# K and V transfers that read HBM in pieces of 48 KB and write rows of 24 KB

## The chip, the cores and the metric

The kernel runs on one core of a Trainium2 chip. The metric is the time of one execution on the device, in microseconds. Runs of one kernel agree within about 0.1%.

## The reference

Four attention blocks run one after the other (A, B, A, B), each for a single new token against a cache of 8192 keys. There are 32 heads of 192 elements, the model width is 640, and everything is bf16.

```python
def block(x, k_cache, v_cache, wq, wo):            # x: 1 x 1 x 640
    q = layernorm(x) @ wq                          # 32 heads of 192
    scores = einsum("bhqd,bhkd->bhqk", q, k_cache) * 192 ** -0.5   # 8192 keys a head
    o = einsum("bhqk,bhkd->bhqd", softmax(scores), v_cache)
    return x + o @ wo                              # wo: 6144 x 640
# x = A(x); x = B(x); x = A(x); x = B(x)
```

Each head of each block needs 3 MB of K and 3 MB of V once. That is 805 MB in 256 transfers, and the weights wq and wo add 63 MB.

## The kernel before

Every engine has a list of instructions with explicit semaphores. For each head, the SyncE queue loads K into one of three buffers and V into one of three others. A buffer is 128 partitions x 24 KB, so each partition holds 64 keys. VectorE multiplies K by the head's query and sums it (ScalarE sums 8 of the 64 rows). After the softmax, TensorE multiplies with V and then with wo.

```python
def sp_k(h, Kt=Kt):
    i = counters["k"] % NKSLOT                 # three buffers
    counters["k"] += 1
    SP.wait(T["kslot"][i])                     # until the buffer's last reader is done
    def f(s, i=i, h=h):
        return s.dma_start(kslot[i][:, :], Kt[0, h].rearrange("(p j) d -> p (j d)", p=128))
    return i, SP.op(f, sem=semK[i], inc=16)
# sp_v is the same for V
...
def sp_wo(g, WO=WO):                           # 768 rows of wo, for four heads
    ...
        return s.dma_start(wo_buf[s_][:, 0:NT, :], WO[r0:r0 + NT * 128, :].rearrange("(t p) n -> p t n", p=128))
...
JA = min(JJ, cfg.get("act_rows", 8))           # rows of the 64 that ScalarE sums
```

## Time and profile before

| | before |
|---|---|
| time, median | 2074.88 us |
| DMA queue of the loads, share of 16 engines | 99.3% |
| VectorE busy | 1764.8 us (85%) |
| HBM read over the span | 868 MB at 419 GB/s |

These lines are from the page of the kernel before. The first rows are the span and each engine's busy time. The DMA row gives the busy share of the DMA engines in tenths, in forty equal slices, and the GB/s row gives what they moved. The packet line, the queue of the loads, and one group of VectorE follow. The last two lines are issues of K and V, with their median time from issue to landing in us.

```profile
span 2073.2 us, 24389 instructions
...
PE 1158.3 (56%) x9625; PEld 915.1 (44%) x9668; DVE 1764.8 (85%) x1190; ACT 596.1 (29%) x3254; POOL 3.1 (0%) x13
...
DMA  9999999999999999999999999999999999999995
GB/s 395 430 425 428 422 422 427 426 430 419 423 426 425 427 422 424 426 426 428 418 423 426 423 429 424 422 427 426 426 410 425 425 423 424 423 423 425 426 427 254
DMA packets 77813, 869.79 MB, mean 420 GB/s; under 512 B 4994, under 2 KB 29572, under 8 KB 44932
...
q1 hardware_dynamic: 77700, 868.24, 99.3%
...
L463 DVE TENSOR_TENSOR kslot<-kslot,q_sb 128x12288 bf16<-128x12288 bf16 x128 | 839.3, 6557 | 226.2 <-DMA kslot<-in_A_k_cache_dram 116.6
...
kslot<-in_A_k_cache_dram SPq DMA_DIRECT2D x64, 3072.0 KB, 32.6
vslot<-in_A_v_cache_dram SPq DMA_DIRECT2D x64, 3072.0 KB, 36.1
...
```

The DMA engines are busy in every slice but the last. A transfer lands 33 to 36 us after it was issued, while moving 3 MB takes about 7.3 us (an estimate: 3.15 MB at the 431 GB/s that stretches with K and V packets alone show). So four or five transfers are always queued, and the engines hardly ever lack work.

The view of the waits of the same kernel (who waited for whom: us in total, times, longest) shows that VectorE waits for K:

```profile
...
DVE kslot L463 <- DMA kslot<-in_A_k_cache_dram: 116.6, 56, 8.2
DVE kslot L463 <- DMA kslot<-in_B_k_cache_dram: 96.6, 49, 6.8
...
```

The trace also records every DMA packet. Over all records of the queue of the loads, sorted by size:

```
kernel  bytes   packets   median ns   sum / 16 engines, us
before  24576     32768         915                 1881.2   K and V
before   2048     15360          87                   85.2   wq
before   1280     24578          58                   90.5   wo
```

One packet of K or V is 24 KB, a whole row of a partition. There are 128 per transfer, so eight for each of 16 engines if they are dealt evenly (the records name no engine).

### The profile page before, as it was taken

The numbers are of one execution on the slowest core, as the hardware profiler recorded it, in microseconds if no ns is written. First come the engines' busy times: TensorE is split into PE (matmuls) and PEld (weight loads), VectorE is DVE, ScalarE is ACT, GpSimd is POOL, SyncE is SP. The second block draws the span as 40 slices with busy tenths as digits, with TensorE's granted clock in tenths as the row PEclk, the third lists the DMA queues.
The fourth block names the chain that finished last, engine by engine and source line by source line (L and its number), as shares of the span: only waits on it lengthen the run. The fifth ranks groups of instructions, "written<-read, shape, count | busy, mean of one in ns | idle before, by whom it ended". The sixth has DMA issues, their size and how long they took to land.

```text
span 2073.2 us, 24389 instructions
## 1 busy us (share of the span) xinstructions
PE 1158.3 (56%) x9625; PEld 915.1 (44%) x9668; DVE 1764.8 (85%) x1190; ACT 596.1 (29%) x3254; POOL 3.1 (0%) x13
## 2 busy tenths in 40 slices
PE   2565556555465555566536565556563665556656
PEld 1444444444354444444425454445452454444444
DVE  7888888988698888898779888889878988888896
ACT  2222232232232322232223332223222332223232
POOL 0000000000000000000000000000000000000000
PEclk7777777877678777777767777777776777777877
DMA  9999999999999999999999999999999999999995
GB/s 395 430 425 428 422 422 427 426 430 419 423 426 425 427 422 424 426 426 428 418 423 426 423 429 424 422 427 426 426 410 425 425 423 424 423 423 425 426 427 254
DMA packets 77813, 869.79 MB, mean 420 GB/s; under 512 B 4994, under 2 KB 29572, under 8 KB 44932
## 3 DMA queue, kind: packets, MB, share of 16 engines
q1 hardware_dynamic: 77700, 868.24, 99.3%
q8 instruction: 76, 1.25, 0.2%
q14 instruction: 37, 0.30, 0.0%
HBM read 868.22 MB, written 0.00 MB: 419 GB/s over the span
## 4 chain that ended last, share of the span: by engine, by line
DMA 45%; issue 25%; DVE 24%; PE 4%; ACT 1%; SPq 1%; POOL 0%; POOLq 0%; DVEq 0%; ACTq 0%
DMA kslot<-in_B_k_cache_dram 28%; DMA kslot<-in_A_k_cache_dram 17%; DVE kslot L463 12%; DVE kslot L504 5%; DVE kslot L492 4%; PE OB L557 3%; DVE s_sb L508 1%; SPq L312 0%; DVE M_sb L530 0%; DVE m_sb L515 0%; PE QB L412 0%; PE YL L632 0%; ACT p_sb L547 0%; DVE rl_sb L572 0%; SPq L295 0%
## 5 line engine op out<-in xcount | busy, mean ns | idle before, releaser
L463 DVE TENSOR_TENSOR kslot<-kslot,q_sb 128x12288 bf16<-128x12288 bf16 x128 | 839.3, 6557 | 226.2 <-DMA kslot<-in_A_k_cache_dram 116.6
L557 PE MATMUL OB<-vslot,p_sb 128*1 128x192 bf16 x8192 | 951.1, 294 | 84.3 <-ACT p_sb L547 78.6
L557 PEld LDWEIGHTS OB<-vslot,p_sb 128*1 128x1 bf16 x8192 | 809.6, 101 | 205.7 <-ACT p_sb L547 93.5
L539 PE MATMUL SA<-M_bf,ones_bf 1*128 1x1 bf16 x128 | 22.9, 179 | 689.2 <-ACT M_bf L537 689.2
L504 DVE TENSOR_TENSOR kslot<-kslot 128x2688 bf16<-128x2688 bf16 (+2 forms) x384 | 374.4, 975 | 13.3
L492 DVE TENSOR_TENSOR kslot<-kslot 128x5376 bf16<-128x5376 bf16 x128 | 374.7, 2927 | 0.1
L481 ACT ACTIVATE kslot<-kslot 128x192 bf16<-128x192 bf16 x1024 | 355.3, 348 | 22.2 <-DVE kslot L463 22.2
L539 PEld LDWEIGHTS SA<-M_bf,ones_bf 1*128 1x128 bf16 x128 | 12.4, 97 | 725.0 <-ACT M_bf L537 725.0
L537 ACT ACTIVATE M_bf<-M_sb 1x1 bf16<-1x1 f32 x128 | 26.5, 207 | 666.3 <-DVE M_sb L530 666.3
L481 ACT ACTIVATION_READ_ACCUMULATOR kslot<-kslot 128x1 f32 x1024 | 192.1, 188 | 0.0
L508 DVE TENSOR_REDUCE s_sb<-kslot 128x56 f32<-128x672 bf16 x128 | 109.1, 852 | 4.4
L632 PE MATMUL YL<-wo,oT_sb 128*1 128x512 bf16 x256 | 83.0, 378 | 51.8 <-ACT oT_sb L609 31.7
L605 ACT ACTIVATE oT_sb<-OB 128x1 bf16<-128x1 f32 x64 | 11.2, 175 | 310.9 <-PE OB L593 310.9
L608 ACT ACTIVATE oT_sb<-OB 64x1 bf16<-64x1 f32 x64 | 10.9, 170 | 281.0 <-PE OB L597 281.0
L412 PE MATMUL QB<-wq,xT_b 128*128 128x512 bf16 x197 | 57.5, 426 | 11.2 <-issue 6.4
L523 PE MATMUL SA<-ident,m_bf 128*1 128x128 bf16 x128 | 28.2, 221 | 54.5 <-ACT m_bf L520 54.5
L632 PEld LDWEIGHTS YL<-wo,oT_sb 128*1 128x1 bf16 x256 | 20.7, 81 | 79.7 <-ACT oT_sb L609 37.2
L634 PE MATMUL YH<-wo,oT_sb 128*1 128x128 bf16 x256 | 55.9, 218 | 0.0
L425 ACT ACTIVATE q_sb<-QB 128x512 bf16<-128x512 f32 x48 | 28.7, 598 | 93.6 <-PE QB L412 93.6
L578 ACT ACTIVATE orow_bf<-OB,rl_sb 1x192 bf16<-1x192 f32 x128 | 51.0, 399 | 1.7 <-DVE rl_sb L572 1.7
L547 ACT ACTIVATE p_sb<-s_sb,negm_sb 128x64 bf16<-128x64 f32 x128 | 44.8, 350 | 4.1
L530 DVE TENSOR_REDUCE M_sb<-SA 1x1 f32<-1x128 f32 x128 | 34.7, 271 | 12.6 <-PE SA L523 12.6
(50 smaller groups left out, 368.9 us busy)
## 6 DMA issues: line engine op xcount, KB each, us to landing
kslot<-in_A_k_cache_dram SPq DMA_DIRECT2D x64, 3072.0 KB, 32.6
vslot<-in_A_v_cache_dram SPq DMA_DIRECT2D x64, 3072.0 KB, 36.1
kslot<-in_B_k_cache_dram SPq DMA_DIRECT2D x64, 3072.0 KB, 32.6
vslot<-in_B_v_cache_dram SPq DMA_DIRECT2D x64, 3072.0 KB, 36.3
wq<-in_A_wq_dram SPq DMA_DIRECT2D x12, 1280.0 KB, 24.9
wo<-in_A_wo_dram SPq DMA_DIRECT2D x16, 960.0 KB, 38.2
wq<-in_B_wq_dram SPq DMA_DIRECT2D x12, 1280.0 KB, 25.7
wo<-in_B_wo_dram SPq DMA_DIRECT2D x16, 960.0 KB, 38.6
```

What stands on the lines that cost most here:

```text
L412: return t.matmul(QB[nb % 2][:, 0:ncols], lhsT=xT_b[:, c, :], rhs=wq_buf[s_][:, c, (nb % 2) * 512:(nb % 2) * 512 + ncols], start=(c == 0), ...
L463: e = DV.op(lambda v, k3=k3, qb_ap=qb_ap: v.tensor_tensor(k3, k3, qb_ap, ALU.mult))
L481: ea = AC.op(lambda a, k3=k3, par=par, j=j: a.activation(k3[:, j, :], k3[:, j, :], ACT.Copy, accum_out=s_sb[par][:, j:j + 1]))
L492: e = DV.op(lambda v, kt=kt, hw_=hw_: v.tensor_tensor(kt[:, :, 0:hw_], kt[:, :, 0:hw_], kt[:, :, hw_:DH], ALU.add))
L504: e = DV.op(lambda v, kt=kt, hw_=hw_, w=w: v.tensor_tensor(kt[:, :, 0:hw_], kt[:, :, 0:hw_], kt[:, :, hw_:w], ALU.add))
L508: cur["s"] = DV.op(lambda v, kt=kt, par=par, w=w, JA=JA: v.tensor_reduce(s_sb[par][:, JA:JJ], kt[:, :, 0:w], AX.X, ALU.add))
L539: cur["negM"] = PE.op(lambda t, par=par: t.matmul(SA[par][:, SA_NEGM:SA_NEGM + 1], lhsT=ones_bf[0:1, 0:128], rhs=M_bf[par][0:1, 0:1], star ...
L547: cur["p"] = AC.op(lambda a, par=par: a.activation(p_sb[par][:], s_sb[par][:], ACT.Exp, bias=negm_sb[par][:], scale=C))
L557: return t.matmul(OB[par][0:1, 0:DH], lhsT=p_sb[par][:, j:j + 1], rhs=vs3[:, j, :], start=(j == 0), stop=(j == JJ - 1))
L578: cur["orow"] = AC.op(lambda a, par=par: a.activation(orow_bf[par][:], OB[par][0:1, 0:DH], ACT.Copy, scale=rl_sb[par][0:1, 0:1]), tag=(f"O ...
L632: return t.matmul(YL[0:1, 0:512], lhsT=lhsT, rhs=rhs[:, 0:512], start=st, stop=sp_)
L634: return t.matmul(YH[0:1, 0:D - 512], lhsT=lhsT, rhs=rhs[:, 512:D], start=st, stop=sp_)
```

## The change

The source of a K or V transfer is described as 64 rows of 48 KB, while the destination keeps 128 rows of 24 KB. Row r of the source is what goes to partitions 2r and 2r + 1, so every byte lands where it did. The author built the instruction by hand. The intent is half as many pieces to read, and with them less fixed cost.

```diff
--- before.py
+++ after.py
@@ -113,6 +113,13 @@
         return bad
 
 
+def wide(nc, e, out, in_):
+    inst = mybir.InstDMACopy(mode="Copy", name=nc.get_next_instruction_name(), engine=e.engine,
+                             ins=list(e.lower_ap_dma(in_)), outs=list(e.lower_ap_dma(out)),
+                             queue="qSPDynamicHW", ant_dge_precooked=False)
+    return e.add_instruction(inst)
+
+
 def build(nc, A_x, A_k, A_v, A_wq, A_wo, B_x, B_k, B_v, B_wq, B_wo, out, dbg=None, cfg=None):
     cfg = dict(cfg or {})
     dbg = dict(dbg or {})
@@ -309,7 +316,7 @@
                 counters["k"] += 1
                 SP.wait(T["kslot"][i])
                 def f(s, i=i, h=h):
-                    return s.dma_start(kslot[i][:, :], Kt[0, h].rearrange("(p j) d -> p (j d)", p=128))
+                    return wide(nc, s, kslot[i][:, :], Kt[0, h].rearrange("(p j) d -> p (j d)", p=64))
                 return i, SP.op(f, sem=semK[i], inc=16)
 
             def sp_v(h, Vt=Vt):
@@ -317,7 +324,7 @@
                 counters["v"] += 1
                 SP.wait(T["vslot"][i])
                 def f(s, i=i, h=h):
-                    return s.dma_start(vslot[i][:, :], Vt[0, h].rearrange("(p j) d -> p (j d)", p=128))
+                    return wide(nc, s, vslot[i][:, :], Vt[0, h].rearrange("(p j) d -> p (j d)", p=64))
                 return i, SP.op(f, sem=semV[i], inc=16)
 
             ev_wq = [None] * NPAIR
```

## The prediction

> **What bounds the kernel.** The DMA engines do. On the profile's page the DMA row of the forty slices reads 9 throughout until the last slice, the DMA queue of the K/V/weight loads is busy for 99.3% of 16 engines' span, and 868 MB at 419 GB/s is the whole span of 2073 us. VectorE, the next busiest, is at 1765 us (85%). The longest real wait of VectorE is for K transfers (116.6 + 96.6 us in the waits view). K and V are 256 transfers of 3 MB, 805 MB, 93% of the bytes. They land 32.6 to 36.3 us after issue, 4 to 5 times what one takes to move, so the queue is always several transfers deep.
>
> The trace's packet records show how little is left: 32768 packets of 24576 B (8 per engine per transfer), median 915 ns, summing to 1881 us per engine. Stretches in which only such packets run move 430.6 GB/s (median), 428.5 (mean). [...] Packets of 2048 B take 87 ns and those of 1280 B 58 ns. A line through the three sizes gives about 0.0368 ns per byte plus about 11 ns a packet (estimate).
>
> **What the change does.** The bytes, their order and their places are the same: rows of 48 KB in HBM are two neighbouring partitions of 24 KB. Each engine reads 4 pieces instead of 8 and still writes 8. If a packet goes with a read piece, 256 x 4 = 1024 packets fewer per engine at about 10 to 11 ns each: some 10 us off the DMA time. If the fixed part goes with the write side, nothing. Nothing is added on VectorE, TensorE or ScalarE. The hand-built instruction may take the SyncE queue a little longer to issue (0.33 us shortest now), but that queue waits over 1 ms for free buffers, so this is hidden.
>
> **Critical path.** The DMA stream runs without gaps from about 2 to 2058 us, so nearly all of what it saves shows in the span; the last 15 us (last head's compute, output) stay. VectorE at 13.8 us a head keeps up with 16.0. I expect 9 us less: 2066 us, range 2056 to 2086. Over 2% faster is nearly excluded[...]: chance 0.02. Within 2%: 0.80. Slower by over 2%: 0.18.
>
> **What would make it wrong.** [...] Fewer than 16 engines [...] I don't expect. [...]
>
> **What the profile would show.** Right: DMA packets drop from 77813 to about 61400, K/V packets are 48 KB and take about 1820 ns; pure K/V stretches run at about 433 GB/s; the DMA row stays 9; VectorE busy stays 1765 us and its waits for K fall by some 10 us; K landing falls slightly. Wrong by no effect: packets fewer, but each over 1830 ns, GB/s unchanged at 424. [...]

On the sum: 1024 packets fewer for each engine at about 10 to 11 ns (estimate from the packet times 915, 87 and 58 ns) came to some 10 us, and the forecast was 9 us less, 2066 us.

## The result

The time is 2074.98 us (median of 4 runs, 2074.16 to 2075.83), against 2074.78 us for the kernel before in the same rounds. The ratio is 0.9999, with a 95% interval of 0.9985 to 1.0013. Ratios here are the mean time of one kernel's fast runs over that of the other's of the same rounds, so they are not quite the ratio of the quoted medians. The interval leaves room for a gain of 3 us, not for 9.

The same lines of the page of the changed kernel (its line numbers are 7 higher):

```profile
span 2072.3 us, 24432 instructions
...
PE 1157.5 (56%) x9668; PEld 912.9 (44%) x9668; DVE 1765.3 (85%) x1190; ACT 593.2 (29%) x3254; POOL 3.1 (0%) x13
...
DMA  9999999999999999999999999999999999999995
GB/s 395 431 430 427 423 424 426 424 429 415 425 427 428 429 421 422 428 428 423 419 427 425 422 425 422 422 428 425 423 421 423 428 422 421 426 422 428 426 425 255
DMA packets 61429, 869.79 MB, mean 420 GB/s; under 512 B 4994, under 2 KB 29572, under 8 KB 44932
...
q1 hardware_dynamic: 61316, 868.24, 99.2%
...
L470 DVE TENSOR_TENSOR kslot<-kslot,q_sb 128x12288 bf16<-128x12288 bf16 x128 | 839.3, 6557 | 226.1 <-DMA kslot<-in_A_k_cache_dram 115.4
...
kslot<-in_A_k_cache_dram SPq DMA_DIRECT2D x64, 3072.0 KB, 32.6
vslot<-in_A_v_cache_dram SPq DMA_DIRECT2D x64, 3072.0 KB, 38.0
...
```

And its waits of VectorE for K:

```profile
...
DVE kslot L470 <- DMA kslot<-in_A_k_cache_dram: 115.4, 55, 7.8
DVE kslot L470 <- DMA kslot<-in_B_k_cache_dram: 97.8, 51, 6.8
...
```

The change did what it says. There are 16384 packets fewer (77813 to 61429), which is 64 per transfer. But the GB/s row, VectorE's waits and the landing of K (32.6 us) have not moved; V lands one to two microseconds later (38.0 against 36.1 us for A, 37.2 against 36.3 for B), without a cost that shows. The packet records say the same:

```
kernel  bytes   packets   median ns   sum / 16 engines, us
before  24576     32768         915                 1881.2
after   49152     16384        1829                 1877.4
```

A packet of twice the size takes twice the time (2 x 915 = 1830). In microsecond-wide stretches that hold K and V packets only, with each packet's bytes spread evenly over its time, the median rate is 431.0 GB/s before and 430.8 after. The sum of the packets' times did fall by 3.8 us, or 0.2%. That is not time won: the loads alone, below, show the same small fall in the records (from 7.344 to 7.325 us per 3 MB) while their pace stays at 7.304 and 7.303 us. So the pace of the stream did not change, and there was nothing that a later wait could have swallowed.

### The profile page after: what moved, and what is told of

It reads as the page before. It is cut to its first block, busy times and chain, and to the rows that moved or that the text cites. A ratio compares the mean times of both kernels' runs of the same rounds, so it can differ in the third digit from the quotient of the medians.

```text
span 2072.3 us, 24432 instructions
## 1 busy us (share of the span) xinstructions
PE 1157.5 (56%) x9668; PEld 912.9 (44%) x9668; DVE 1765.3 (85%) x1190; ACT 593.2 (29%) x3254; POOL 3.1 (0%) x13
## 2 busy tenths in 40 slices
DMA packets 61429, 869.79 MB, mean 420 GB/s; under 512 B 4994, under 2 KB 29572, under 8 KB 44932
## 4 chain that ended last, share of the span: by engine, by line
DMA 45%; issue 25%; DVE 24%; PE 4%; ACT 1%; SPq 0%; POOL 0%; POOLq 0%; DVEq 0%; ACTq 0%
DMA kslot<-in_B_k_cache_dram 28%; DMA kslot<-in_A_k_cache_dram 15%; DVE kslot L470 12%; DVE kslot L511 5%; DVE kslot L499 5%; PE OB L564 3%; DMA vslot<-in_A_v_cache_dram 2%; DVE s_sb L515 1%; PE QB L419 0%; DVE M_sb L537 0%; DVE m_sb L522 0%; PE YL L639 0%; ACT p_sb L554 0%; DVE rl_sb L579 0%; ACT M_bf L544 0%
## 5 line engine op out<-in xcount | busy, mean ns | idle before, releaser
L419 PE MATMUL QB<-wq,xT_b 128*128 128x512 bf16 x240 | 67.1, 419 | 3.7 <-ACT xT_b L397 3.7
## 6 DMA issues: line engine op xcount, KB each, us to landing
kslot<-in_A_k_cache_dram SPq DMA_DIRECT2D x64, 3072.0 KB, 32.6
kslot<-in_B_k_cache_dram SPq DMA_DIRECT2D x64, 3072.0 KB, 32.6
vslot<-in_B_v_cache_dram SPq DMA_DIRECT2D x64, 3072.0 KB, 37.2
```

The source lines that it names most:

```text
L419: return t.matmul(QB[nb % 2][:, 0:ncols], lhsT=xT_b[:, c, :], rhs=wq_buf[s_][:, c, (nb % 2) * 512:(nb % 2) * 512 + ncols], start=(c == 0), ...
```

## The experiments

Three theories of a packet's fixed part, and one doubt, had to be told apart:

- READ (the prediction's): about 11 ns go with each piece that is read.
- WRITE: they go with each piece that is written. The change left 128 of those.
- RATE: there is no fixed part at these sizes, only a pace per byte of about 430 GB/s (431.0 measured above).
- The doubt: something other than the DMA stream (VectorE, or the return of buffers) holds the time, so that a small saving would not show.

Each theory can be tested by the write side. The opposite test, reads smaller than writes, was not run: two such copies, rows of 24 KB read in pieces of 12 KB, did not compile.

A word on correctness. With the given inputs the attention adds so little to x that a kernel which returns x unchanged passes the comparison. So "correct" says little about layouts here. The kernels before and after, e_w6, e_wo3 and e_wo3_r48 were therefore also run in a functional simulation with 8 heads and larger values, where attention makes up most of the output. All five gave the same agreement with the reference (correlation 0.9999). It was repeated, with e_r6w6 added, and all six agreed equally well.

### Loads alone, in twelve shapes (m_phases)

All compute is gone. The SyncE queue loads 100.7 MB in each of twelve stretches, each drained before the next. The output is x, wrong.

```python
def single(p, r, q):      # 3 MB, read in p * r pieces; each row of 24 KB is written in q pieces
    src = srcs[t // 8][0, t % 8].rearrange("(p j) d -> p (j d)", p=p)
    # r > 1: src.rearrange("p (r n) -> p r n", r=r), dst.rearrange("p (q n) -> p q n", q=q)
single(128, 1, 1); single(64, 1, 1); double()      # double: two heads, 6 MB, rows of 48 KB
single(64, 2, 2); single(16, 8, 2); single(64, 2, 4); single(128, 4, 4); ...
```

> Loads alone, no compute, output wrong on purpose (it is x). Twelve stretches of 100.7 MB each (32 transfers of 3 MB, or 16 of 6 MB), each drained before the next; they differ only in the size of the pieces read and written. 1: read 24 KB, write 24 KB. 2: 48/24. 3: 48/48. 4: 24/12. 5: 24/12[...]. 6: 24/6. 7: 6/6. 8: 24/1.5. 9: 6/1.5. 10: 1.5/1.5. 11: 48/3. 12: as 1. Theory READ (the prediction's: about 11 ns per piece read): 2 faster than 1 by 0.6%; 3 as 2; 6 as 1, 7 slower by 3.4%; 8 as 1; 10 slower by 16%. Theory WRITE (about 11 ns per piece written): 2 as 1; 3 faster by 0.6%; 6 and 7 both 3.4% slower; 8, 9 and 10 all 16% slower. Theory RATE (a limit per byte, about 430 GB/s; no fixed cost that shows at these sizes): 1 to 8 all alike, 3 no faster than 1; 10 slower at most because its packets are small. [...]

For stretch 5 it expected 10% or more above stretch 4, or else the same.

The timeline of SyncE's queue in this kernel, one line per source tensor (start in us, us, what was issued). From one line's start to the next, eight transfers of 3 MB were issued (four of 6 MB in the stretch of 48/48), each as soon as an older one had freed its buffer. The pairs of lines are, in order: 24 KB read and 24 KB written, 48/24, 48/48, 24/12, 24/12 described in another way, 24/6, and 1.5/1.5.

```profile
...
25.90 51.61 SPq L16 DMA_DIRECT2D big<-in_A_v_cache_dram  x8
84.34 51.60 SPq L16 DMA_DIRECT2D big<-in_B_k_cache_dram  x8
...
262.61 51.59 SPq L16 DMA_DIRECT2D big<-in_A_v_cache_dram  x8
321.04 51.60 SPq L16 DMA_DIRECT2D big<-in_B_k_cache_dram  x8
...
506.98 44.07 SPq L16 DMA_DIRECT2D big<-in_A_v_cache_dram  x4
565.11 44.07 SPq L16 DMA_DIRECT2D big<-in_B_k_cache_dram  x4
...
736.21 52.25 SPq L16 DMA_DIRECT2D big<-in_A_v_cache_dram  x8
795.23 52.25 SPq L16 DMA_DIRECT2D big<-in_B_k_cache_dram  x8
...
998.96 105.77 SPq L16 DMA_DIRECT2D big<-in_A_v_cache_dram  x8
1119.21 105.79 SPq L16 DMA_DIRECT2D big<-in_B_k_cache_dram  x8
...
1461.81 60.19 SPq L16 DMA_DIRECT2D big<-in_A_v_cache_dram  x8
1522.05 60.19 SPq L16 DMA_DIRECT2D big<-in_B_k_cache_dram  x8
...
2523.41 67.42 SPq L16 DMA_DIRECT2D big<-in_A_v_cache_dram  x8
2590.87 67.42 SPq L16 DMA_DIRECT2D big<-in_B_k_cache_dram  x8
...
```

The distance between such starts gives the pace. This table takes it over 16 transfers of 3 MB (50.3 MB), from the second line of a stretch to the fourth:

| stretch | KB read / written | pieces written per engine in 3 MB | us per 3 MB | ns per further written piece, against stretch 1 |
|---|---|---|---|---|
| 1 | 24 / 24 | 8 | 7.304 | |
| 2 | 48 / 24 | 8 | 7.303 | |
| 3 | 48 / 48 | 4 | 7.267 | 9.2 |
| 4 | 24 / 12 | 16 | 7.378 | 9.2 |
| 6 | 24 / 6 | 32 | 7.529 | 9.4 |
| 7 | 6 / 6 | 32 | 7.532 | |
| 11 | 48 / 3 | 64 | 7.830 | 9.4 |
| 8, 9, 10 | 24, 6, 1.5 / 1.5 | 128 | 8.433 | 9.4 |
| 5 | 24 / 12, other description | 16 | 15.03 | |
| 12 | 24 / 24 again | 8 | 7.306 | |

This is one run, but stretch 12 repeats stretch 1 within 0.002 us, and the smallest difference that is used here, 0.037 us for stretch 3, is far above that. READ falls and so does RATE. The size of the pieces read makes no difference, from 48 KB down to the written size, while every piece written costs 9.4 ns of its engine, if the pieces are dealt evenly over 16 (128 - 8 = 120 pieces more cost 1.129 us). Taking 8 x 9.4 ns off stretch 1 leaves 7.229 us for 196,608 B per engine, which is 435.2 GB/s for sixteen (an estimate from these two numbers). Stretch 3 is the counterpart of the change: widening the written side as well does gain 0.5% (7.267 us against 7.304).

What is not told apart is whether a read piece has a cost of its own, hidden beside the write. It can only be said that it is not above 9.4 ns down to 1.5 KB, for reads and writes of equal number show no more than the writes (7.532 us in stretch 7 against 7.529 in stretch 6). Nor is it told apart whether the writing as such counts, or simply the finer of the two cuts: in every run the written pieces were at least as many as the read ones, and all of them went into SBUF.

Stretches 4 and 5 have the same sizes. In 5 the source is described as 16 x 8 pieces instead of 64 x 2. It takes 2.04 times as long (15.03 against 7.378 us per 3 MB). It is not that fewer packets were under way: in the middle of stretch 5 the packets' times fill 16 engines as in stretch 4 (share 1.00 in both, and the page's DMA row reads 9 while its GB/s fall to 209), but one packet of 24 KB takes 1925 ns (median) against 926. The author took this for engines that collide, but the trace names no engine per packet, so the cause is not shown. The change itself did not fall into it: stretch 2 is as fast as stretch 1 (7.303 against 7.304 us).

### Written pieces of 6 KB in the whole kernel (e_w6, e_r6w6)

```diff
-wide(nc, s, kslot[i][:, :], Kt[0, h].rearrange("(p j) d -> p (j d)", p=64))
+wide(nc, s, kslot[i][:, :].rearrange("p (q n) -> p q n", q=4), Kt[0, h].rearrange("(p q j) d -> p q (j d)", p=64, q=2))   # e_w6
+wide(nc, s, kslot[i][:, :].rearrange("p (q n) -> p q n", q=4), Kt[0, h].rearrange("(p q j) d -> p q (j d)", p=128, q=4))  # e_r6w6
```

V is changed in the same way.

> The whole kernel, K and V read in pieces of 24 KB as before, but each row of 24 KB is written in four pieces of 6 KB (24 write pieces more per engine and transfer). WRITE: 24 x 11 ns x 256 = 68 us slower, about 2140 us. READ: as before, 2075. RATE: as before, 2075.

> The whole kernel, K and V both read and written in pieces of 6 KB (32 each per engine and transfer, against 8). READ: 68 us slower, about 2140 us. WRITE: about 2140 us. RATE: 2075 us, or a few us more.

Measured: e_w6 took 2130.56 us (ratio 1.0266, 1.0249 to 1.0283) and e_r6w6 took 2130.97 us (1.0269, 1.0254 to 1.0285), against 2074.96 us. Lines of the page of e_w6:

```profile
span 2129.2 us, 24389 instructions
...
GB/s 388 416 414 416 411 411 416 416 415 408 414 414 414 415 412 414 413 415 416 407 414 412 413 416 414 413 414 415 414 401 413 414 412 414 408 414 413 415 415 251
DMA packets 77813, 869.79 MB, mean 409 GB/s; under 512 B 4994, under 2 KB 29572, under 8 KB 44932
...
```

And of the page of e_r6w6:

```profile
span 2129.8 us, 24389 instructions
...
DMA packets 176117, 869.79 MB, mean 408 GB/s; under 512 B 4994, under 2 KB 29572, under 8 KB 176004
...
```

Both are about 56 us slower, and they differ by less than half a microsecond, although e_w6 has as many packets as the kernel before (77813) and e_r6w6 has 98304 more. The number of packets is the number of pieces read, and it means nothing for the time here. At 9.4 ns per written piece the estimate is 24 x 256 x 9.4 ns = 57.8 us. The 68 us came from the prediction's 11 ns. In the packet records the 24 KB packets of e_w6 take 945 ns (median) against 915: three written pieces more in a packet of the same bytes.

### VectorE relieved (e_act16)

```diff
-                JA = min(JJ, cfg.get("act_rows", 8))
+                JA = min(JJ, cfg.get("act_rows", 16))
```

> The kernel before with 16 instead of 8 of the 64 rows per partition summed on ScalarE, which takes about a seventh of the sum tree off VectorE (some 120 us of 1765) and adds about 550 us to ScalarE. If the DMA stream bounds the kernel, as all three theories of the packets assume: no change, 2075 us within 0.3%. If instead VectorE or the return of buffers by VectorE held the stream back, so that a faster DMA could not show: faster by 1% or more.

Measured: 2086.48 us, ratio 1.0054 (1.0039 to 1.0069), which is neither of the two. Lines of its page:

```profile
span 2084.8 us, 26437 instructions
...
PE 1160.4 (56%) x9625; PEld 920.7 (44%) x9668; DVE 1656.5 (79%) x1190; ACT 946.3 (45%) x5302; POOL 3.1 (0%) x13
...
L515 DVE TENSOR_REDUCE m_sb<-s_sb 128x1 f32<-128x64 f32 x128 | 28.2, 220 | 86.7 <-ACT kslot L481 86.5
...
```

VectorE lost 108 us of work and the kernel became 11.5 us slower, so VectorE's amount of work does not bound it. The last line points to the harm. VectorE's maximum over a head's scores (line 515), after which the K buffer is free, now waits 86.5 us in total for ScalarE's sums; in the kernel before it waits for nothing. The view of windows shows two stretches, around the end of the third block and within the last, where the DMA rate sags (the columns end with the DMA share and GB/s). First e_act16:

```profile
...
core 0: us, PE busy (x) PEld busy (x) DVE busy (x) ACT busy (x) POOL busy (x), PEclk, DMA share, GB/s
1530.00:1580.00 50.00, 31.07 (x240) 22.89 (x241) 27.96 (x28) 18.32 (x96) 0.54 (x1) 0.73 0.93 386
1755.00:1800.00 45.00, 21.37 (x178) 16.80 (x178) 34.72 (x24) 18.98 (x107) 0.00 (x0) 0.73 0.96 397
...
```

Then the kernel before, in the same windows:

```profile
...
core 0: us, PE busy (x) PEld busy (x) DVE busy (x) ACT busy (x) POOL busy (x), PEclk, DMA share, GB/s
1530.00:1580.00 50.00, 24.00 (x189) 16.90 (x187) 30.89 (x27) 12.05 (x60) 0.54 (x1) 0.72 0.98 407
1755.00:1800.00 45.00, 23.65 (x200) 18.68 (x198) 35.55 (x24) 9.85 (x56) 0.00 (x0) 0.75 1.00 415
...
```

The DMA share falls to 0.93 and 0.96 there, where the kernel before has 0.98 and 1.00. These two stretches account for about 5 of the 11.5 us. Counted by the bytes landed, e_act16 is 2.6 us behind the kernel before at 1540 us, 6.1 at 1600 and 7.8 at 1805; about 4 us more come after 2000 us, where the last V load is issued 11.4 us later (at 2038.1 against 2026.6 us). So the kernel before is bound by the DMA stream, but that stream seems only just fed: work that VectorE gave up won nothing, and buffers that came back later seem to have cost time. That it is the buffers' return that starves the stream is argued from the order of waits; no run here separates it from ScalarE's delay of the softmax, which holds V buffers too.

### Fewer written pieces in wo (e_wo3, e_wo3_r48)

If WRITE holds, the place to save is wherever small pieces are written. wo is written in pieces of 1280 B. Three neighbouring rows on one partition make one piece of 3840 B. The attention output then has to be laid on the partitions in the same order: for each head, 64 partitions x 3.

```diff
-return s.dma_start(wo_buf[s_][:, 0:NT, :], WO[r0:r0 + NT * 128, :].rearrange("(t p) n -> p t n", p=128))
+return s.dma_start(wo_buf[s_][:, :, :], WO[r0:r0 + NT * 128, :].rearrange("(a p s) n -> p a (s n)", p=128, s=3))
...   # o to partitions: three matmuls of every third element, one copy
+lo = 64 * par
+for c in range(3):
+    t.matmul(ob_[lo:lo + 64, OB_OT + c:OB_OT + c + 1], lhsT=orf[0:1, c:DH:3], rhs=one, ...)
+a.activation(ot[lo:lo + 64, 0:3], ob_[lo:lo + 64, OB_OT:OB_OT + 3], ACT.Copy)
...   # times wo: three pairs of matmuls instead of two
+mm = [(ot[:, c:c + 1], wob[:, i // 2, c * D:(c + 1) * D]) for c in range(3)]
```

e_wo3 has K and V as before; e_wo3_r48 has the change on top.

> K and V as in the kernel before. The output weights wo are laid three rows to a partition, so each is written in pieces of 3840 B instead of 1280 B (and read so): 512 write pieces fewer in each of 32 transfers, 32 per engine, at 9.4 ns as the stretches of the loads alone gave: 32 x 32 x 9.4 ns = 9.6 us of DMA time less. WRITE: 2065 us, about 0.5% faster. RATE: no change, 2075. It also tells whether 10 us taken off the DMA stream show in the time at all, which the prediction took for granted: if the stream were held back by the return of buffers, this would stay at 2075 too.

> The same with the change on top (K and V read in pieces of 48 KB, written in rows of 24 KB). WRITE: no different from the kernel with wo alone, 2065 us within 0.1%. READ: 10 us less than that, 2055.

Measured: e_wo3 took 2065.31 us (ratio 0.9954, 0.9940 to 0.9967) and e_wo3_r48 took 2065.35 us (0.9956, 0.9943 to 0.9968), against 2074.78 us. Lines of the page of e_wo3:

```profile
span 2063.7 us, 24944 instructions
...
PE 1198.0 (58%) x9988; PEld 936.1 (45%) x9988; DVE 1765.2 (86%) x1190; ACT 590.7 (29%) x3126; POOL 3.1 (0%) x13
...
GB/s 398 431 427 429 426 427 429 428 429 422 427 429 426 429 425 425 428 428 430 418 427 429 425 427 427 425 430 428 427 411 427 428 426 426 429 424 429 429 428 246
DMA packets 61430, 869.82 MB, mean 421 GB/s; under 512 B 4994, under 2 KB 4996, under 8 KB 28548
...
```

And of the page of e_wo3_r48:

```profile
span 2063.2 us, 24944 instructions
...
DMA packets 45046, 869.82 MB, mean 422 GB/s; under 512 B 4994, under 2 KB 4996, under 8 KB 28548
...
```

The gain is 9.5 us where WRITE said 9.6 (an estimate), and the change on top adds nothing, with another 16384 packets fewer. This also answers the doubt: ten microseconds taken off the DMA stream arrive in the time nearly whole, in spite of 40 us more work on TensorE (1198.0 us busy against 1158.3). Nor did the new layout win the time at the end of the kernel: the last V packet ends 9.5 us earlier (at 2048.0 us against 2057.5), and about 15.7 us of the span follow it in both. e_wo3 is faster than both kernels by 0.5%, which is clear of the noise though far below 2%. Its read pieces shrank in number as well, so e_wo3 alone does not tell READ from WRITE (READ, at 11 ns, would give 11 us). The stretches do that, for reads down to 1.5 KB, and so does e_wo3_r48: READ said 2055 us for it.

## Why the prediction was wrong

- "The DMA engines do" bind the kernel: right. More DMA work (e_w6) and less (e_wo3) both show in the time almost one for one, and less work on VectorE does not help.
- "About 11 ns a packet": the size was near (9.4 ns).
- "If a packet goes with a read piece ... some 10 us off the DMA time. If the fixed part goes with the write side, nothing." This is the step that failed: what a packet's fixed time belongs to. The packets did go with the read pieces, as their number shows, and I took the fixed time of a packet for a cost of the packet. The cost is of the written piece, 9.4 ns each, and the change left those alone: 48 KB read and 24 KB written took 7.303 us per 3 MB against 7.304. The prediction named both cases and bet on the first without evidence: in the kernel before, every packet has exactly one read and one written piece, so its trace can't tell them apart.
- "K/V packets ... take about 1820 ns; pure K/V stretches run at about 433 GB/s; ... waits for K fall by some 10 us": wrong. They take 1829 ns, run at 430.8 GB/s, and the waits are 213.2 us before and after. The signature that it gave for "no effect" (fewer packets, "each over 1830 ns", GB/s unchanged at 424) is what the profile shows, but for 1 ns.
- "Nearly all of what it saves shows in the span": right, as e_wo3 shows with 9.5 of an estimated 9.6 us.
- The loss of over 2% that was given a chance of 0.18 did not occur (2074.98 us against 2074.78), and in the loads alone 64 pieces took 7.303 us per 3 MB against 7.304. A description of the pieces that makes loads 2.04 times as long exists (stretch 5, 15.03 us against 7.378); its cause is not shown.
- The longer issue of the hand-built instruction was hidden, as said: the median for K went from 0.52 (A) and 0.38 (B) to 0.47 us, on a queue that waits for buffers.

The time lay inside the stated range and within 2%, as given the best chance, but the gain of 9 us was not there.

## What to carry to other kernels

When a load is bound by the DMA engines, count the contiguous pieces that each engine writes, not the packets or the reads: here each written piece cost 9.4 ns beside its bytes, whatever the reads looked like (loads into SBUF, with reads of 1.5 to 48 KB that were no smaller than the writes). A fixed cost read from a trace belongs to nothing in particular until one thing has been varied without the other, so vary the two sides separately before building on it. The gain then lay in the smallest written rows (the 1280 B rows of wo, 4% of the bytes) and not in the 93% of the bytes that already came in rows of 24 KB.
